# Two products of the output stage in couples of k-blocks, each behind a direct part

## The chip, the core and the metric

The kernel runs on one core of a Trainium2 chip. Its metric is the time of one execution on the device in microseconds (us). The engines named below: TensorE (PE in the profile; PEld is its weight load), VectorE (DVE), ScalarE (ACT), GpSimd (POOL, which here only issues DMAs), and SyncE (SP, whose queue issues the loads).

## The reference

All arrays are float32, with 2048 rows of x, D = 1024 and F = 3584.

```python
def _A_ref(x, dft_seq_re, dft_seq_im, dft_hid_re, dft_hid_im):
    a = jnp.einsum("bsd,ed->bse", x, dft_hid_re)
    b = jnp.einsum("bsd,ed->bse", x, dft_hid_im)
    return jnp.einsum("ts,bse->bte", dft_seq_re, a) - jnp.einsum("ts,bse->bte", dft_seq_im, b)

def _B_ref(x, w1, b1, w2, b2):
    h = jnp.einsum("bsd,df->bsf", x, w1) + b1
    r = jnp.where(h > 0, h, 0)
    h = r * r
    return jnp.einsum("bsf,fd->bsd", h, w2) + b2

g = _sigmoid((x * gate_w).sum(-1, keepdims=True))
return g * a + (1 - g) * b        # a = _A_ref(...), b = _B_ref(...)
```

## The kernel before

**Four stages.** The X stage multiplies x by the two hidden DFT matrices (`ab`), the C stage multiplies that by the two sequence DFT matrices and by g, and keeps the result in DRAM (`gy`). The H stage, in two parts, makes h, squared and rectified, and keeps it in DRAM (`h_far`). The output stage, `o_stage`, multiplies w2 by h (contraction 3584), adds b2, multiplies by 1 - g, adds `gy` and stores. It comes last and is the stage that the change touches. Its result has 8 x 128 rows (D) and 2048 columns.

**Fast multiplication.** Every stage is one 2x2 block product done with seven block products instead of eight (Winograd's form). `SUMS_L` and `SUMS_R` hold the sums of blocks (S1 to S4 of the left, T1 to T4 of the right), `FACTORS` says which factors each product 1 to 7 takes: 1 is (0,0)x(0,0), 2 is (0,1)x(1,0), 3 is S4x(1,1), 4 is (1,1)xT4, 5 is S1xT1, 6 is S2xT2, 7 is S3xT3. `seven` runs the products in the order 1, 2, 5, 6, 3, 7, 4 and says what they are added to: 1 makes `one`; 2 adds to `one` and ends the result block c11; 5 begins c22; 6 adds to `one` and makes `u` and c12; 3 ends c12; 7 adds to `u` and ends c22; 4 adds to `u` and ends c21, the kernel's last result.

**A product.** In the C and output stages (`tall`) the contraction of one block product is cut into `ksteps` k-blocks of 256, 8 in the C stage and 7 in the output stage. An operand is a tile of 128 partitions x 2 x 512 in float32. It is split into `hi` (rounded to fp32r by ScalarE, L220) and `lo` (the rest, by VectorE, L230), each in a slot of its own, and a product of two operands is hi x hi + hi x lo + lo x hi. A step takes one left operand (512 rows) and one right operand (512 columns): 4 row tiles x 2 halves of k x 3 = 24 matmuls of 128x512 into PSUM. A direct product (`direct`) is 7 k-blocks x 2 column halves c = 14 steps in the output stage.

**The second level.** `twice` does 2k of a product's k-blocks once more by seven products. A couple is two neighbouring k-blocks (j = 0, 1); the left operand is cut into two halves of 256 rows (`View`), the right has its two column halves. So a couple takes 7 steps of 12 matmuls, where a direct one takes 4 steps of 24. For that VectorE makes four more sums on each side (L172), 128x512 on the left and 128x1024 on the right, and there are seven left operands of 128x512 (`hi` and `lo` side by side in one slot, `both`) and seven right ones. All couples run a first pass (partial products 1, 6, 7, 5, each added up over the couples), then a second pass (2, 4, 3, added in PSUM onto what the first pass left). What the first pass leaves is taken up by VectorE: when something is already there (`old`), partial product 1 costs a copy of ScalarE and one addition, 6 and 7 two additions each, 5 three. The k-blocks that belong to no couple (`rest`) are done directly; before the change they come last, in half steps of 12 matmuls that go into the same PSUM groups as the second pass (`to`, `own`).

`TWICE_C = {2: 4, 3: 3, 4: 2}` and `TWICE_O = {2: 3, 3: 3}` give the number of couples for each product of the C and the output stage. A direct product 6 also makes `early` the sums T4 of those k-blocks that product 4 needs in couples (L456, L360): T4 is stored to DRAM and loaded again later, where otherwise T2 is stored and T4 is made from the loaded T2 in product 4.

**PSUM.** A `Group` is a set of row tiles added up over some steps; `banks` holds four pools of two banks each. With `onto`, ScalarE first copies the earlier value into PSUM (L293). A finished pair of row tiles goes to `put` (a copy by ScalarE, L432, or `final`) or `add` (VectorE, L438). `final` in the output stage is two scalar_tensor_tensor (L831) and one addition (L834) by VectorE and a store from POOL's queue (L936). The kernel's last block ends by `last` instead, row tile by row tile (`by_row`; L818, L820, stores at L821 from SP's and ACT's queues). An addition of `five` that ends a block has its final made `LATER` = 3 steps on.

**The order of the work** is written by a planner that runs at build time. `steps` is the list of steps in TensorE's order. For each step i, loads are issued up to `LOADS` = 12 steps ahead when there are free slots (55 slots of SBUF in all, some kept back), sums and conversions must be in VectorE's and ScalarE's queues `SUMS` = 3 and `RESTS` = 2 steps ahead of their use, and go up to `SPREAD` = 9 steps ahead where the planner's own clock for VectorE still has room within the present step and slots are free. Each engine then works through its queue in order.

Of the kernel before, what the change touches and what calls it, by code (L numbers as in the profile page):

```python
# [16 lines left out]
NF = F // P  # L17
SLOTS, KEEP, RAWS = 55, 5, 4
WIDE, TALL_C, TALL_O = ((1, 2, 5, 6, 3, 7, 4),) * 3
TWICE_X, TWICE_C, TWICE_O = (1, 2, 5, 3, 4), {2: 4, 3: 3, 4: 2}, {2: 3, 3: 3}  # L20
LATER = 3
WARM = 44
FAR_TALL, FAR_WIDE = ("T2",), ()
TWICE_H = (1, 2, 5, 3, 4), (2, 5, 3, 4)
# [17 lines left out]
def gated_mix_kernel(ctx: ExitStack, tc: tile.TileContext, x4, xn, w4, ct, w1a, w1b, w2, b1, b2, gw, out):  # L42
# [276 lines left out]
    def step(st, mv, group):  # L319
        st.uses += 1  # L320
        mv.uses += 1
        steps.append((st, mv, group, []))
        needs = 0
        count[group] = count.get(group, 0) + 1
        if count[group] % group.k == 0:
            needs += group.done[count[group] // group.k - 1][1]
        wanted.append(needs)
# [81 lines left out]
                    ends[e] = len(steps)  # L409
        return ends  # L410

    def tall(left, right, ksteps, order, second, target, final, last=None):

# [42 lines left out]

        def twice(p, old, new, ends, drop, sign):

            l, r = FACTORS[p]
            k = second[p]
            rest = range(2 * k, ksteps)
            more = len(rest)
            tmp = {key: Near("u") for key in ((0, 0),)}

            def block(m, c):
                return c, m

            def near(b):  # L470
                return b if isinstance(b, Near) else Part(b)

            base = {(j, q): near(left[2 * q + j].of(l)) for j in range(2) for q in range(k)}
            l2 = {q: Sums(lambda m, j, q=q: View(base[j, q], 256 * m), SUMS_L, True) for q in range(k)}
            r2 = {q: Sums(lambda j, c, q=q: right[2 * q + j, c].of(r), SUMS_R, True) for q in range(k)}

            def one(_, ps):
                if old:
                    tmp[0, 0].new()
                    nc.scalar.activation(flat(tmp[0, 0].slot), flat(ps), AF.Copy)  # L480
                    add(new, block(0, 0), ps, src=old)
                    if drop:
                        old[block(0, 0)].drop()
                else:
                    put(new, block(0, 0), ps)

            def onward(dst, key, ps):

                if old:
                    u = tmp[0, 0].slot  # L490
                    nc.vector.tensor_tensor(flat(u), flat(u), flat(ps), op=ADD)
                    at = new[key].slot or new[key].new()
                    nc.vector.tensor_tensor(flat(at), flat(old[key].slot), flat(u), op=ADD)
                    vec(2 * (VEC[0] + VEC[1]))
                    new[key].begun = True
                    if drop:
                        old[key].drop()

            def six(_, ps):
                if old:  # L500
                    onward(new, block(0, 1), ps)
                else:
                    add({block(0, 1): new[block(0, 1)]}, block(0, 1), ps, src={block(0, 1): new[block(0, 0)]})

            def seven_(_, ps):
                if old:
                    onward(new, block(1, 0), ps)
                else:
                    add({block(1, 0): new[block(1, 0)]}, block(1, 0), ps, src={block(1, 0): new[block(0, 1)]})

            def five(_, ps):
                key = block(1, 1)
                add(new, block(0, 1), ps)
                if old:
                    at = new[key].slot or new[key].new()
                    nc.vector.tensor_tensor(flat(at), flat(old[key].slot), flat(ps), op=ADD)
                    if drop:
                        old[key].drop()
                    nc.vector.tensor_tensor(flat(at), flat(at), flat(tmp[0, 0].slot), op=ADD)
                    vec(2 * (VEC[0] + VEC[1]))  # L520
                    tmp[0, 0].drop()
                    new[key].begun = True
                    if ends and not more:
                        new[key].done = True
                        later.append((now[0] + LATER, lambda: final(new[key], None)))
                else:
                    add({key: new[key]}, key, ps, ends and not more, src={key: new[block(1, 0)]})

            fresh = old is not new
            groups = {1: Group(2, k, (one, fresh + bool(old), [new[block(0, 0)]])),  # L530
                      6: Group(2, k, (six, fresh, [new[block(0, 1)]])),
                      7: Group(2, k, (seven_, fresh, [new[block(1, 0)]])),
                      5: Group(2, k, (five, fresh, [new[block(1, 1)], new[block(0, 1)]]))}
            for q in range(k):
                for p2 in (1, 6, 7, 5):
                    l_, r_ = FACTORS[p2]
                    step(l2[q].operand(l_, 256), r2[q].operand(r_), groups[p2])

            def to(m, c):
                key = block(m, c)  # L540
                if last and p == order[-1] and (m, c) == (1, 1):
                    return Group(2, more, (lambda _, ps, row: last(new[key], ps, row), 0, [new[key]]),
                                 onto=[new[key]], by_row=True)
                return Group(2, k * ((m, c) != (1, 1)) + more, (lambda _, ps: put(new, key, ps, ends), 0, [new[key]]),
                             onto=[new[key]])

            groups = {2: to(0, 0), 3: to(0, 1), 4: to(1, 0), None: to(1, 1)}
            for q in range(k):
                again = Sums(lambda j, c, q=q: right[2 * q + j, c].of(r), SUMS_R, True)
                again.made.update({key: r2[q].of(key) for key in ("T1", "T2")})  # L550
                for p2 in (2, 4, 3):
                    l_, r_ = FACTORS[p2]
                    step(l2[q].operand(l_, 256), again.operand(r_), groups[p2])
            own = []
            for q in rest:
                st = left[q].operand(l)
                for c in range(2):
                    mv = right[q, c].operand(r)
                    own += [(Half(st, 256 * m), mv, groups[{(0, 0): 2, (0, 1): 3, (1, 0): 4}.get((m, c))])
                            for m in range(2)]  # L560
            if last and p == order[-1]:
                own.sort(key=lambda e: e[2] is groups[None])
            for e in own:
                step(*e)
# [215 lines left out]
    def c_stage():  # L780
        rows = [Row(n, False) for n in range(2)]
        to = {}

        def target(i, n, k):
            near = Near("y")
            to[near] = i, n, *k
            return near

        def final(dst, ps):
            i, n, c, rp = to[dst]  # L790
            nc.vector.tensor_tensor(dst.slot, dst.slot if ps is None else ps, rows[n].of(c).broadcast_to([P, 2, 512]),
                                    op=ALU.mult)
            vec(VEC[0] + VEC[1])
            rows[n].used()
            stores.append((gy[i, n, c, rp], dst, 0, 2))

        at = len(steps)
        tall(lambda i, j, q: ab[j, q, i], lambda j, n, q, c: ct[n, c, j, q], 8, TALL_C, TWICE_C, target, final)
        return at, rows


    def o_stage():
# [10 lines left out]
        def last(dst, ps, k):  # L813
            i, n, c, rp = to[dst]
            e, t, add = 4 * i + 2 * rp + k, 1024 * n + 512 * c, fetched[i, n, c, rp]
            dst.slot or dst.new()
            at = dst.slot[:, k, :]
            nc.vector.scalar_tensor_tensor(at, ps[:, 0, :], b2c[:, e:e + 1], rows[n].of(c)[:, 0, :], op0=ALU.add,  # L818
                                           op1=ALU.mult)
            nc.vector.tensor_tensor(at, at, add.slot[:, k, :], op=ADD)  # L820
            (nc.scalar if k else nc.sync).dma_start(out[e * P:(e + 1) * P, t:t + 512], at)  # L821
            if k:
                rows[n].used()
                add.used()
                dst.drop()
# [14 lines left out]

        fetched = {}
        at = len(steps)
        ends = tall(lambda i, j, q: w2[i, j, q], lambda j, n, q, c: h_far[j, q, 2 * n + c], 7, TALL_O, TWICE_O, target, final, last)
        return at, rows, fetched, ends

    def want(k, *items):
# [10 lines left out]
    at, rows, fetched, ends = o_stage()  # L857
# [7 lines left out]
    n = len(steps)  # L865
# [138 lines left out]
```

## Time and profile before

| | us |
|---|---|
| median of 3 runs | 1891.29 (1889.42 to 1892.37) |
| the profiled execution | 1888.96 |
| its span, first to last instruction | 1886.9 |
| granted TensorE clock, mean | 0.999 |

The page's second part cuts the span into 40 slices of 47 us and shows the busy share of each in tenths, and the share of the DMA engines:

```profile
PE   9999999999999999999999999999999999999998
DVE  8997898599777998798896997989976997789882
ACT  6474564363343554455484797767954434264440
DMA  5732989339786489383551865628872887629971
```

A row of groups reads: line, engine, operation, out<-in, shape, xcount | busy us in all, mean ns of one | idle us just before them, and what ended it. A row of the timeline reads: start, length, engine, line, operation, count. A row of windows reads: the stretch and its length, then for PE, PEld, DVE, ACT and POOL the busy us and the number of instructions, then the clock, the DMA share and GB/s. A row of waits reads: who waited for whom, us in all, times, the longest.

### The profile page before, as it was taken

To read this page: it belongs to the slowest core of one execution; us is meant where nothing else is said; L and a number is where in the kernel's file an instruction comes from. 1 tells how busy PE (TensorE), PEld (TensorE's weight loads), DVE (VectorE), ACT (ScalarE), POOL (GpSimd) and SP (SyncE) were. 2 spreads that over 40 slices of the span, in tenths; PEclk is the share of its full clock that TensorE was granted. 3 is DMA by queue.
4 is the path that set the end of the run, shared out by engine and by line. 5 is a ranking of instruction groups with operands and counts; after the bars stand their busy time and mean duration, and the time that the engine had idled before them with its cause. 6 is when DMAs were issued, how large, how long until landed. Compare 5 with 4: busy or idle time off the path is not lost.

```text
span 1886.9 us, 21962 instructions
## 1 busy us (share of the span) xinstructions
PE 1876.6 (99%) x8288; PEld 1551.3 (82%) x8288; DVE 1610.3 (85%) x1543; ACT 1001.3 (53%) x1123; POOL 86.8 (5%) x161
## 2 busy tenths in 40 slices
PE   9999999999999999999999999999999999999998
PEld 7888888888888888888888888888888888888887
DVE  8997898599777998798896997989976997789882
ACT  6474564363343554455484797767954434264440
POOL 0000110000010000000000000000100001000000
PEclk9999999999999999999999999999999999999999
DMA  5732989339786489383551865628872887629971
GB/s 223 247 121 86 348 288 412 129 117 375 261 312 256 151 322 383 139 312 112 170 198 56 325 228 195 228 84 299 293 259 97 317 336 265 218 103 370 409 300 45
DMA packets 128425, 442.93 MB, mean 235 GB/s; under 512 B 14128, under 2 KB 23616, under 8 KB 128320
## 3 DMA queue, kind: packets, MB, share of 16 engines
q1 hardware_dynamic: 106416, 363.26, 53.0%
q0 software_dynamic: 21472, 77.61, 10.3%
q8 instruction: 65, 1.06, 0.2%
q10 hardware_dynamic: 432, 0.66, 0.1%
q14 instruction: 40, 0.33, 0.1%
HBM read 362.83 MB, written 78.65 MB: 234 GB/s over the span
## 4 chain that ended last, share of the span: by engine, by line
PE 97%; DVE 2%; ACT 0%; DMA 0%; issue 0%; SPq 0%; DVEq 0%; ACTq 0%
PE ps L306 97%; DVE lo L230 1%; DVE h L603 0%; DVE sum L172 0%; DMA raw<-in_w 0%; DVE o L818 0%; ACT u L596 0%; ACT hi L220 0%; DVE o L820 0%; DVE raw L172 0%; SPq L152 0%; DVEq L172 0%; DVEq L230 0%; ACTq L596 0%
## 5 line engine op out<-in xcount | busy, mean ns | idle before, releaser
L306 PE MATMUL ps<-hi 128*128 128x512 f32 x2328 | 905.7, 390 | 4.0 <-ACT hi L220 3.6
L306 PE MATMUL ps<-lo,hi 128*128 128x512 f32 x2328 | 905.3, 389 | 0.0
L306 PE MATMUL ps<-hi,lo 128*128 128x512 f32 x2328 | 904.2, 389 | 0.1
L220 ACT ACTIVATE hi<-raw 128x1024 fp32r<-128x1024 f32 (+2 forms) x413 | 420.6, 1037 | 399.0 <-DVE raw L172 274.1
L230 DVE TENSOR_TENSOR lo<-raw,hi 128x1024 fp32r<-128x1024 f32 (+2 forms) x413 | 484.5, 1199 | 57.5 <-ACT hi L220 31.3
L306 PEld LDWEIGHTS ps<-hi 128*128 128x128 f32 x2328 | 437.2, 188 | 95.9 <-ACT hi L220 4.2
L306 PEld LDWEIGHTS ps<-hi,lo 128*128 128x128 f32 x2328 | 437.1, 188 | 92.0 <-DVE lo L230 1.0
L306 PEld LDWEIGHTS ps<-lo,hi 128*128 128x128 f32 x2328 | 437.3, 188 | 91.0 <-DVE lo L230 0.4
L172 DVE TENSOR_TENSOR raw<-raw 128x1024 f32<-128x1024 f32 (+1 forms) x276 | 326.4, 1207 | 56.4 <-DMA raw<-in_ct 19.4
L220 ACT ACTIVATE hi<-sum 128x1024 fp32r<-128x1024 f32 (+1 forms) x172 | 176.1, 1036 | 184.8 <-DVE sum L172 151.2
L306 PE MATMUL ps<-hi,both 128*128 128x512 f32 x840 | 259.8, 389 | 0.0
L230 DVE TENSOR_TENSOR lo<-sum,hi 128x1024 fp32r<-128x1024 f32 (+1 forms) x172 | 203.3, 1198 | 32.9 <-PE ps L306 16.6
L306 PEld LDWEIGHTS ps<-hi,both 128*128 128x128 f32 x840 | 157.7, 188 | 33.8 <-ACT ps L293 0.7
L306 PE MATMUL ps<-lo,both 128*128 128x512 f32 x420 | 163.5, 389 | 0.0
L172 DVE TENSOR_TENSOR sum<-raw 128x1024 f32<-128x1024 f32 (+1 forms) x116 | 121.9, 1066 | 35.4 <-PE ps L306 28.1
L172 DVE TENSOR_TENSOR sum<-raw,sum 128x1024 f32<-128x1024 f32 (+2 forms) x87 | 96.8, 1119 | 12.0 <-PE ps L306 11.7
L603 DVE TENSOR_TENSOR h<-h,ps 128x1024 f32<-128x1024 f32 x92 | 98.2, 1086 | 9.6 <-ACT u L596 7.1
L596 ACT ACTIVATE u<-ps 128x1024 f32<-128x1024 f32 x76 | 71.9, 950 | 62.0 <-PE ps L306 54.3
L306 PEld LDWEIGHTS ps<-lo,both 128*128 128x128 f32 x420 | 78.8, 188 | 16.1
L293 ACT ACTIVATE ps<-u 128x1024 f32<-128x1024 f32 (+1 forms) x74 | 70.0, 953 | 22.2 <-DVE o L831 12.0
L700 ACT ACTIVATE h<-h,b1c 128x512 f32<-128x512 f32 x112 | 74.3, 712 | 6.3 <-DVE h L603 6.0
L220 ACT ACTIVATE both<-sum 128x512 fp32r<-128x512 f32 x60 | 37.1, 625 | 52.7 <-DVE sum L172 33.4
(61 smaller groups left out, 650.5 us busy)
## 6 DMA issues: line engine op xcount, KB each, us to landing
raw<-in_ct SPq DMA_DIRECT2D x151, 512.0 KB, 6.2
raw<-h SPq DMA_DIRECT2D x132, 512.0 KB, 7.3
raw<-in_x SPq DMA_DIRECT2D x107, 512.0 KB, 5.3
raw<-in_w SPq DMA_DIRECT2D x98, 512.0 KB, 6.3
raw<-ab SPq DMA_DIRECT2D x72, 512.0 KB, 6.8
h<-h POOLq DMA_DIRECT2D x48, 512.0 KB, 5.7
raw<-in_w1a SPq DMA_DIRECT2D x36, 512.0 KB, 5.0
ab<-ab POOLq DMA_DIRECT2D x32, 512.0 KB, 6.7
```

The lines of the kernel that those rows point to most:

```text
L172: nc.vector.tensor_tensor(self.slot[:, k, c], src[0][:, k, c], src[1][:, k, c], op=self.op)
L220: nc.scalar.activation(self.hi[:, k, c], self.block.slot[:, k, c], AF.Copy)
L230: nc.vector.tensor_tensor(self.lo[:, k, c], self.block.slot[:, k, c], self.hi[:, k, c].bitcast(F32), op=SUB)
L293: nc.scalar.activation(t[:, :n, :], b.slot[:, at:at + n, :], AF.Copy, scale=self.sign)
L306: nc.tensor.matmul(self.ps[r // self.per][:, r % self.per, :], a[:, kk, r * P:(r + 1) * P], b[:, kk, :], start=self.at == 1 and kk + n == ...
L596: nc.scalar.activation(view(near.slot, k), view(ps, k), AF.Copy, scale=float(sign))
L603: nc.vector.tensor_tensor(view(near.slot, k), view((src or dst)[k].slot, k), view(ps, k), op=ADD if sign > 0 else SUB)
L700: nc.scalar.activation(dst.slot[:, k, :], (dst.slot if ps is None else ps)[:, k, :], AF.Relu, bias=b1c[:, tile0 + k:tile0 + k + 1])
```

## The change

`TWICE_O` gets two couples for product 1 and two for product 4. With `FIRST_C = (2,)` and `FIRST_O = (2, 4)`, `twice` does the k-blocks outside the couples first, as whole steps of 24 matmuls in two groups of four row tiles, when there is no earlier value (`not old`, product 1) or the product is in `first`; the sums of these steps are put into the product's own blocks by ScalarE, and the couples then go on from them as their `old`. This holds for products 1, 2 and 4 of the output stage; product 3 keeps its k-block at the end. In the C stage product 2 has no k-block outside its couples, and product 4 isn't in `FIRST_C`.

In product 4, the last, the steps of the second pass are sorted so that partial product 4 comes behind 2 and 3, and the block (1, 0) that it ends goes row tile by row tile through `last`. Before, that was the second column half of the direct product, two blocks of two row tiles each.

As product 4 now has couples, product 6 of the output stage makes T4 early for k-blocks 0 to 3, both column halves.

```diff
-TWICE_X, TWICE_C, TWICE_O = (1, 2, 5, 3, 4), {2: 4, 3: 3, 4: 2}, {2: 3, 3: 3}
+TWICE_X, TWICE_C, TWICE_O = (1, 2, 5, 3, 4), {2: 4, 3: 3, 4: 2}, {1: 2, 2: 3, 3: 3, 4: 2}
 LATER = 3
+FIRST_C, FIRST_O = (2,), (2, 4)
...
-    def tall(left, right, ksteps, order, second, target, final, last=None):
+    def tall(left, right, ksteps, order, second, first, target, final, last=None):
...
             k = second[p]
             rest = range(2 * k, ksteps)
+            if rest and (not old or p in first):
+                some = [Group(4, len(rest), (lambda rp, ps, c=c: put(new, (c, rp), ps, sign=sign), 2 * (old is not new),
+                                             [new[c, rp] for rp in range(2)]),
+                              onto=old and [old[c, rp] for rp in range(2)], spend=drop) for c in range(2)]
+                sts = {q: left[q].operand(l) for q in rest}
+                for q in rest:
+                    for c in range(2):
+                        step(sts[q], right[q, c].operand(r), some[c])
+                old, rest, drop = new, (), False
             more = len(rest)
...
-                if last and p == order[-1] and (m, c) == (1, 1):
-                    return Group(2, more, (lambda _, ps, row: last(new[key], ps, row), 0, [new[key]]),
+                if last and p == order[-1] and (m, c) == ((1, 1) if more else (1, 0)):
+                    return Group(2, more or k, (lambda _, ps, row: last(new[key], ps, row), 0, [new[key]]),
                                  onto=[new[key]], by_row=True)
...
+            own = []
             for q in range(k):
                 again = Sums(lambda j, c, q=q: right[2 * q + j, c].of(r), SUMS_R, True)
                 again.made.update({key: r2[q].of(key) for key in ("T1", "T2")})
                 for p2 in (2, 4, 3):
                     l_, r_ = FACTORS[p2]
-                    step(l2[q].operand(l_, 256), again.operand(r_), groups[p2])
+                    own.append((l2[q].operand(l_, 256), again.operand(r_), groups[p2]))
+            if last and p == order[-1] and not more:
+                own.sort(key=lambda e: e[2] is groups[4])
+            for e in own:
+                step(*e)
...
-        ends = tall(lambda i, j, q: w2[i, j, q], lambda j, n, q, c: h_far[j, q, 2 * n + c], 7, TALL_O, TWICE_O, target, final, last)
+        ends = tall(lambda i, j, q: w2[i, j, q], lambda j, n, q, c: h_far[j, q, 2 * n + c], 7, TALL_O, TWICE_O, FIRST_O, target, final, last)
```

More of the change, by code (lines that the diff above doesn't have):

```diff
@@ L797, in c_stage @@
         at = len(steps)
-        tall(lambda i, j, q: ab[j, q, i], lambda j, n, q, c: ct[n, c, j, q], 8, TALL_C, TWICE_C, target, final)
+        tall(lambda i, j, q: ab[j, q, i], lambda j, n, q, c: ct[n, c, j, q], 8, TALL_C, TWICE_C, FIRST_C, target, final)
         return at, rows
```

## The prediction

> **What bounds the kernel now.** I read the page's head, then PE's waits, then the chain of waits, then a table of windows, one for each of the output stage's seven products (their bounds are counted back from the last matmul: products 1, 2, 5, 6, 3, 7, 4 have 336, 300, 336, 336, 300, 336, 336 matmuls).
>
> ```profile
> span 1886.9 us, 21962 instructions
> PE 1876.6 (99%) x8288; PEld 1551.3 (82%) x8288; DVE 1610.3 (85%) x1543; ACT 1001.3 (53%) x1123; POOL 86.8 (5%) x161
> ...
> PE ps L306 <- ACT hi L220: 3.6, 2, 2.9
> PE ps L898 <- DVE ones L895: 1.1, 1, 1.1
> PE ps L306 <- ACT ps L293: 0.3, 1, 0.3
> ...
> 1300.11 577.56 PE ps L306 x2546
> ```
>
> TensorE sets the time: it waited 5.0 us in the whole execution, and the chain's last piece is 2546 matmuls end to end: 577.56 / 2546 = 0.2268 us each. Fewer matmuls are therefore worth 0.2268 us apiece, as long as the others keep up. VectorE, at 85%, is the one that may not:
>
> ```profile
> core 0: us, PE busy (x) PEld busy (x) DVE busy (x) ACT busy (x) POOL busy (x), PEclk, DMA share, GB/s
> 1364.80:1440.80 76.00, 76.00 (x337) 62.90 (x337) 49.07 (x51) 34.81 (x42) 2.15 (x4) 1.00 0.58 211
> 1440.80:1508.80 68.00, 68.00 (x301) 56.20 (x300) 63.85 (x67) 34.72 (x40) 0.98 (x2) 1.00 0.66 247
> 1508.80:1585.00 76.20, 76.20 (x338) 63.07 (x337) 62.70 (x56) 31.86 (x31) 5.13 (x9) 1.00 0.79 293
> 1585.00:1661.20 76.20, 76.20 (x338) 63.10 (x337) 56.02 (x54) 26.19 (x30) 4.23 (x8) 1.00 0.61 217
> 1661.20:1729.20 68.00, 68.00 (x301) 56.16 (x300) 66.85 (x72) 38.99 (x45) 1.08 (x2) 1.00 0.65 244
> 1729.20:1805.40 76.20, 76.20 (x338) 63.08 (x337) 64.38 (x59) 33.52 (x33) 1.81 (x3) 1.00 0.94 364
> 1805.40:1881.70 76.30, 76.30 (x337) 62.81 (x335) 44.00 (x45) 16.76 (x18) 4.28 (x6) 1.00 0.44 168
> ```
>
> PE is busy for the whole of each window. VectorE is nearly full in the two products that already use the second level (2 and 3: 94% and 98%), and has 26.9 us free in product 1 and 32.3 us in product 4, the two that are changed.
>
> **The change part by part.**
>
> *Matmuls.* Product 1 was 14 steps of 24 matmuls. Now six steps (k-blocks 4 to 6) stay direct, 6 x 24 = 144, and two couples take 2 x 7 steps of 12 = 168: 312 instead of 336. Product 4 likewise. Product 2 keeps its 300 and only does its direct part first. So 48 matmuls go: 48 x 0.2268 = **-10.9 us**. Beyond that nothing can be gained, since PE has no idle time in these windows.
>
> *VectorE's work.* Its prices:
>
> ```profile
> 1367.85 19.39 DVE L230 TENSOR_TENSOR lo<-raw,hi 128x1024 fp32r<-128x1024 f32 x17
> ...
> 1398.98 1.29 DVE L230 TENSOR_TENSOR both<-sum,both 128x512 fp32r<-128x512 f32 x2
> ...
> L438 DVE TENSOR_TENSOR o<-o,ps 128x1024 f32<-128x1024 f32 x11 | 13.4, 1219 | 11.6 <-ACT u L432 7.9 <-PE ps L306 2.7 <-ACT u L480 1.0
> L230 DVE TENSOR_TENSOR both<-raw,both 128x512 fp32r<-128x512 f32 x18 | 12.3, 688 | 0.0
> ```
>
> A row of one instruction overlaps the next by a little: (19.39 - 1.22) / 16 = 1.14 us from start to start for 128x1024, 1.29 - 0.69 = 0.60 for 128x512; an addition out of PSUM lasts as long as the first kind. A couple done directly takes six rests lo, 6 x 1.14 = 6.8. By the second level it takes 4 sums and 7 rests on the left, 11 x 0.60 = 6.6, and 4 sums and 7 rests on the right, 11 x 1.14 = 12.5: 12.3 more, 24.6 for two couples. Taking up the seven partial products (1 addition, then 2, 2 and 3) is 8 x 1.14 = 9.1. So each of products 1 and 4 costs VectorE **33.7 us more**.
>
> *Products 1, 2 and 5.* Free time of VectorE: 26.9 + 4.2 + 13.5 = 44.6; less the 5.4 that PE becomes shorter, 39.2, against 33.7. It fits over the three. Over 1 and 2 alone it doesn't: 31.1 - 5.4 = 25.7, that is 8.0 short. What may slide from 2 into 5 are the finals of product 2 and the first operands of product 5. Product 2's direct part first also helps: 10.9 us of PE with three rests to make. So the stall lies between 0 and 8.0; I take **+2.0**, near the lower end, as the window of product 3 went at 98% without a wait of PE. Whether the free time of product 1 can be used is the open point. There VectorE stood before tiles whose slot PE had not released:
>
> ```profile
> DVE sum L172 <- PE ps L306: 16.5, 9, 3.9
> ACT both L220 <- PE ps L306: 8.8, 3, 4.6
> ```
>
> (the waits between 1381 and 1460 us). All 55 slots were taken, because the 21 operands of product 1, two slots each, had been prepared far ahead: the row of 17 rests above ends at 1387, while PE read the last of them after 1430. With only nine direct operands, 18 slots, that hoard becomes smaller, and the couples' first operands can be made from about 1378 on, 19 us before their step at 1397. So I expect it to be usable.
>
> *Products 6 and 4.* `early` makes 8 of the 14 sums T4 in product 6 and sends them out and back; the same number of T2 copies is no longer stored for them, and loads only move (8 more in product 6, 8 fewer later). 8 x 1.14 = 9.1 us of VectorE goes from 4 into 6, where 20.2 are free. Product 4 then has 44.0 + 33.7 - 9.1 = 68.6 in 70.9, and product 7 before it has 11.8 free. The nearest case is product 4 of the C stage, which already is two couples with early T4, with PE as busy:
>
> ```profile
> 791.90:873.60 81.70, 81.70 (x361) 67.37 (x360) 77.82 (x72) 40.81 (x43) 3.19 (x6) 1.00 0.67 245
> ```
>
> 77.8 of 81.7 and no wait. One place is new: sorted for the last block, the second pass runs 2, 3, 2, 3, 4, 4, so group 3 begins one step of 12 x 0.2268 = 2.7 us after the fourth partial product, and needs VectorE's addition (1.22) and ScalarE's copy back into PSUM at L293 (1.02, the row below) by then. That fits with 0.5 to spare, unless VectorE is two instructions late (2.3 us, so a wait of 1.8). Behind that copy on ScalarE stand the next hi conversions. I take **+0.3** (0 to 1.8).
>
> *ScalarE, queues, loads.*
>
> ```profile
> L293 ACT ACTIVATE ps<-u 128x1024 f32<-128x1024 f32 x62 | 63.3, 1023 | 18.2 <-DVE o L831 8.0 <-DVE y L791 4.3 <-DVE h L603 3.0
> L220 ACT ACTIVATE hi<-sum 128x1024 fp32r<-128x1024 f32 x156 | 163.3, 1056 | 175.6 <-DVE sum L172 144.2 <-PE ps L306 16.3 <-DMA gy<-y 5.5
> L220 ACT ACTIVATE both<-sum 128x512 fp32r<-128x512 f32 x60 | 37.1, 625 | 52.7 <-DVE sum L172 33.4 <-PE ps L306 18.9
> ```
>
> A couple's conversions take 7 x 0.63 + 7 x 1.06 instead of 6 x 1.06, 5.4 more; with seven more copies into and out of PSUM at 1.02, product 1 (and 4) asks 18 us more of ScalarE: 53 of 70.6, hidden. Product 2's moved part gives VectorE as many additions as before and ScalarE seven more copies (four blocks put aside, three fetched again), 7.2 on 34.7 of 68; its two steps' loads go to the front of that product on SP's queue, ahead of the couples'. Product 1 loads four right blocks twice, 1.4 us each (512 KB at the 364 GB/s of product 7, an estimate), beside a DMA share of 0.58. On POOL's queue T4 copies replace T2 copies one for one, and are wanted only two products later.
>
> *The end.*
>
> ```profile
> 1877.69 0.75 DVE L818 SCALAR_TENSOR_TENSOR o<-ps,b2c,g 128x512 f32<-128x512 f32 x1 [28.69 <-PE ps L306]
> ...
> 1881.86 0.74 DVE L818 SCALAR_TENSOR_TENSOR o<-ps,b2c,g 128x512 f32<-128x512 f32 x1
> 1882.64 0.69 DVE L820 TENSOR_TENSOR o<-o,raw 128x512 f32<-128x512 f32 x1
> ...
> 1883.36 0.34 ACTq L821 DMA_DIRECT2D out<-o  x1
> ...
> out<-o ACTq DMA_DIRECT2D x2, 256.0 KB, 2.5
> ...
> out<-o POOLq DMA_DIRECT2D x2, 512.0 KB, 3.1
> ```
>
> VectorE was idle 28.7 us before the last four rows; now it works until about 8 us before the end, and only two rows are left to the row-wise path. The last row's two instructions and its store stay as they are. The block before them ends 24 matmuls = 5.4 us earlier, takes 2 x 0.75 + 1.22 = 2.7, and its store by POOL lands 3.1 us after issue (when little else moves, as 35 us before the end), 0.4 us behind the last matmul; the last row's, issued at 1883.36, lands 2.5 us on, 4.1 behind it. **0** (0 to 1).
>
> *Sum* against the profiled execution's own 1888.96 (span 1886.9): -10.9 + 2.0 + 0.3 = -8.6, so 1880.4. That execution was 2.3 us quicker than the median of the runs, 1891.29; on the median's footing the forecast is **1882.7**.
>
> The C stage is built by the same function, but its product 2 has four couples of eight k-blocks and no direct part, and its product 4 isn't in FIRST_C, so nothing moves there.
>
> **The rivals.**
>
> *A. VectorE is short in products 1 and 2, and what could slide doesn't.* Then PE waits 8.0 us, if in one place then with a slower clock behind it:
>
> ```profile
> 14.91 0.80 PE L306 MATMUL ps<-hi 128*128 128x512 f32 x1 [2.91 <-ACT hi L220]
> ...
> 18.14 0.40 PE L306 MATMUL ps<-hi,lo 128*128 128x512 f32 x1
> ```
>
> After a wait of 2.9 us the next seven matmuls took 3.23 us instead of 1.59, 1.6 lost. -10.9 + 8.0 + 1.6 + 0.3 gives 1890.3. For it: the 98% of product 3 leaves no reserve. Against: the nearby free time of product 5. [...]
>
> *B. Slower: the free time of product 1 stays free, because slots and not VectorE set the pace there.* A couple holds sums, both passes' blocks and operands at once, and a step lasts 2.7 us instead of 5.4, so the same number of prepared steps covers half the time. Each us of the 26.9 that can't be used adds to the 8.0. Half unused: 8.0 + 13.5 = 21.5, so 1891.3 - 10.9 + 21.5 + 0.3 = 1902.2. It is slower by over 0.2% once waits exceed 14.7, that is when more than 6.7 of the 26.9 are lost. For it: the waits for slots above. Against: product 2, three couples at once, had only 4.2 us free.
>
> *C. Nothing stalls:* 1880.4, within the forecast's own range.
>
> *D. The matmuls go, but product 4's second pass waits,* VectorE finishing its 68.6 us late: it must be done about 8 us before the end, 68.6 - 8 = 60.6 in 62.9. If product 7 hands over 5 us less than before, 3 us of wait: 1885.4.
>
> **How the numbers follow.** Forecast with C and D's smaller part 0.60, D 0.06, A 0.18, B 0.16. 0.2% (3.8 us) is about what a measurement of this kernel tells from no change. Faster: forecast and D, 0.66. Same: A, 0.18. Slower: B, 0.16. The range goes from 1879 (no stall, and 1.4 for the spread of the runs) to 1893, taking in A and leaving out most of B.
>
> **What would show it.** Right: about 8196 matmuls on PE beside the 44 of the start; products 1 and 4 in 70.8 us each; VectorE over 95% in products 1 and 2; PE's waits in the output stage under 4 us; VectorE idle before the last rows for a few us. Wrong: PE waits for lo or hi in product 1 with VectorE waiting for PE (B), or with VectorE full (A); a wait at L293 in the last 20 us (D).

## The result, and the profile after

| | before | changed |
|---|---|---|
| median of 10 runs each, us | 1890.91 (1889.05 to 1892.37) | 1886.49 (1883.10 to 1890.02) |
| ratio to before | | 0.9977, 95% interval 0.9968 to 0.9986 |
| profiled execution, us (span) | 1888.96 (1886.9) | 1884.27 (1882.3) |

The changed kernel is faster by 0.23%, 4.4 us in the medians, with an interval of 2.6 to 6.0 us. The forecast was 1882.7, 8.6 us under the median known then; the range, 1879 to 1893, holds the result. What is new is the spread: 6.9 us from the quickest run to the slowest, against 3.3 before.

The page's head and PE's waits in the changed kernel:

```profile
span 1882.3 us, 22015 instructions
PE 1868.7 (99%) x8240; PEld 1545.3 (82%) x8240; DVE 1674.7 (89%) x1622; ACT 1039.7 (55%) x1176; POOL 87.5 (5%) x162
...
PE ps L307 <- ACT hi L221: 3.4, 1, 3.4
PE ps L307 <- ACT ps L294: 2.7, 3, 1.8
PE ps L915 <- DVE ones L912: 1.1, 1, 1.1
PE ps L307 <- DVE lo L231: 0.8, 2, 0.6
```

8240 - 44 = 8196 matmuls: the 48 are gone. The waits for PSUM reloads (ACT at L294, the old L293) have grown from 0.3 to 2.7 us. The windows of the output stage's seven products and of the end show where:

```profile
core 0: us, PE busy (x) PEld busy (x) DVE busy (x) ACT busy (x) POOL busy (x), PEclk, DMA share, GB/s
1367.05:1438.84 71.79, 71.13 (x314) 58.45 (x312) 70.41 (x77) 47.58 (x61) 2.15 (x4) 1.00 0.62 213
1438.84:1506.89 68.05, 68.05 (x301) 56.22 (x300) 67.82 (x76) 41.09 (x49) 1.22 (x2) 1.00 0.64 227
1506.89:1583.05 76.16, 76.16 (x337) 63.10 (x336) 70.46 (x63) 32.98 (x32) 3.83 (x7) 1.00 0.88 340
1583.05:1659.21 76.16, 76.16 (x337) 63.10 (x336) 59.19 (x56) 27.84 (x31) 5.33 (x10) 1.00 0.71 268
1659.21:1729.69 70.48, 68.57 (x301) 56.26 (x300) 69.78 (x77) 37.95 (x45) 1.10 (x2) 1.00 0.61 228
1729.69:1805.85 76.16, 76.16 (x337) 63.12 (x336) 64.08 (x59) 33.56 (x33) 1.79 (x3) 1.00 0.95 367
1805.85:1876.57 70.72, 70.72 (x313) 58.42 (x311) 69.54 (x77) 34.81 (x42) 5.00 (x7) 1.00 0.34 122
1876.57:1882.30 5.73, 0.16 (x1) 0.00 (x0) 1.74 (x3) 0.00 (x0) 0.00 (x0) 0.79 0.43 158
```

Each window runs from a product's first matmul to the next product's. Less 0.2268 for each matmul, what is left is what PE lost there: product 1, 71.79 - 312 x 0.2268 = 1.0; product 3, which the change doesn't touch, 70.48 - 300 x 0.2268 = 2.4; all others under 0.1. VectorE is now full in products 1, 2, 3 and 4 (98%, 100%, 99%, 98%).

The spans differ by 4.6 us: -10.9 for the matmuls, +1.0 and +2.4, about +0.4 at the end, and +2.7 in the X stage, which the change doesn't reach, less 0.3 for an earlier first matmul. The experiments put the X stage's part to chance.

**The wait in product 3.** VectorE and ScalarE there, first in the kernel before, then in the changed one. The first pass of product 3 ends 144 matmuls after its beginning, at 1693.8 before and at 1691.9 after.

```profile
1693.13 1.22 DVE L491 TENSOR_TENSOR u<-u,ps 128x1024 f32<-128x1024 f32 x1
1694.26 1.22 DVE L438 TENSOR_TENSOR o<-o,ps 128x1024 f32<-128x1024 f32 x1
1695.39 1.22 DVE L493 TENSOR_TENSOR o<-o,u 128x1024 f32<-128x1024 f32 x1
...
1695.51 1.03 ACT L293 ACTIVATE ps<-o 128x1024 f32<-128x1024 f32 x1 [3.66 <-DVE o L438]
```

```profile
1692.71 1.22 DVE L503 TENSOR_TENSOR u<-u,ps 128x1024 f32<-128x1024 f32 x1
1693.85 1.22 DVE L231 TENSOR_TENSOR lo<-raw,hi 128x1024 fp32r<-128x1024 f32 x1
1694.98 1.22 DVE L505 TENSOR_TENSOR o<-o,u 128x1024 f32<-128x1024 f32 x1
1696.12 1.22 DVE L440 TENSOR_TENSOR o<-o,ps 128x1024 f32<-128x1024 f32 x1
...
1696.29 1.03 ACT L294 ACTIVATE ps<-o 128x1024 f32<-128x1024 f32 x1 [2.59 <-DVE o L505]
...
1695.12 0.50 PE L307 MATMUL ps<-lo,both 128*128 128x512 f32 x1 [0.16 <-DVE lo L231]
1697.37 0.50 PE L307 MATMUL ps<-hi,both 128*128 128x512 f32 x1 [1.75 <-ACT ps L294]
```

Before, the copy into PSUM that the second pass needs first after its own first step begins 1.7 us behind the first pass and is done at 1696.54, just as that step of 12 x 0.2268 = 2.72 us ends. After, it begins 4.4 us behind: an operand's rest (lo at 1693.85) stands between the additions, and the additions come in another order (the source asks for groups 2, 4, 3 in both kernels, but in the built program the second pass of product 3 begins with groups 2, 3, 4 before and 2, 4, 3 after). From one matmul's start to the next 2.3 us pass.

### The profile page after: what moved, and what is told of

Same layout as the page of the kernel before. It is cut to its first block, busy times and chain, and to the rows that moved or that the text cites. A ratio compares the mean times of both kernels' runs of the same rounds, so it can differ in the third digit from the quotient of the medians.

```text
span 1882.3 us, 22015 instructions
## 1 busy us (share of the span) xinstructions
PE 1868.7 (99%) x8240; PEld 1545.3 (82%) x8240; DVE 1674.7 (89%) x1622; ACT 1039.7 (55%) x1176; POOL 87.5 (5%) x162
## 4 chain that ended last, share of the span: by engine, by line
PE 94%; DVE 4%; DMA 1%; issue 0%; ACT 0%; SPq 0%; DVEq 0%; ACTq 0%
PE ps L307 94%; DVE lo L231 1%; DVE sum L173 1%; DVE h L620 0%; DMA raw<-in_x 0%; DMA g<-g_far 0%; DVE both L231 0%; DVE u L503 0%; DVE raw L173 0%; DMA raw<-in_w 0%; DVE o L505 0%; DVE o L440 0%; SPq L153 0%; ACT ps L294 0%; DVE o L835 0%
## 5 line engine op out<-in xcount | busy, mean ns | idle before, releaser
L307 PE MATMUL ps<-hi 128*128 128x512 f32 x2200 | 857.2, 390 | 3.7 <-ACT hi L221 3.4
L307 PE MATMUL ps<-hi,lo 128*128 128x512 f32 x2200 | 856.5, 390 | 0.7 <-DVE lo L231 0.6
L307 PE MATMUL ps<-lo,hi 128*128 128x512 f32 x2200 | 857.0, 390 | 0.0
L307 PEld LDWEIGHTS ps<-hi 128*128 128x128 f32 x2200 | 414.0, 188 | 90.4 <-ACT hi L221 3.8
L307 PEld LDWEIGHTS ps<-lo,hi 128*128 128x128 f32 x2200 | 413.7, 188 | 85.8 <-DVE lo L231 0.3
L307 PE MATMUL ps<-hi,both 128*128 128x512 f32 x1064 | 329.8, 390 | 2.4 <-ACT ps L294 2.4
L307 PEld LDWEIGHTS ps<-hi,both 128*128 128x128 f32 x1064 | 199.9, 188 | 45.6 <-ACT ps L294 4.1
L307 PE MATMUL ps<-lo,both 128*128 128x512 f32 x532 | 207.4, 390 | 0.2 <-DVE lo L231 0.2
L173 DVE TENSOR_TENSOR sum<-raw 128x1024 f32<-128x1024 f32 (+2 forms) x132 | 136.8, 1053 | 18.2 <-PE ps L307 14.2
L294 ACT ACTIVATE ps<-u 128x1024 f32<-128x1024 f32 x79 | 76.8, 979 | 21.5 <-DVE o L848 7.1
L717 ACT ACTIVATE h<-h,b1c 128x512 f32<-128x512 f32 x112 | 74.4, 714 | 6.0 <-DVE h L620 5.6
```

The lines of the kernel that those rows point to most:

```text
L173: nc.vector.tensor_tensor(self.slot[:, k, c], src[0][:, k, c], src[1][:, k, c], op=self.op)
L294: nc.scalar.activation(t[:, :n, :], b.slot[:, at:at + n, :], AF.Copy, scale=self.sign)
L307: nc.tensor.matmul(self.ps[r // self.per][:, r % self.per, :], a[:, kk, r * P:(r + 1) * P], b[:, kk, :], start=self.at == 1 and kk + n == ...
L717: nc.scalar.activation(dst.slot[:, k, :], (dst.slot if ps is None else ps)[:, k, :], AF.Relu, bias=b1c[:, tile0 + k:tile0 + k + 1])
```

## The experiments

All were timed against the kernel before. "Lost" is worked out as above, in the one profiled execution; that of e5 is the quickest of its five runs, that of e11 the slowest.

| kernel | median, us | ratio (95%) | lost in products, us |
|---|---|---|---|
| e1, product 1 alone | 1887.39 | 0.9983 (0.9974 to 0.9992) | 2: 1.3; 3: 1.2 |
| e2, product 4 alone | 1885.15 | 0.9972 (0.9960 to 0.9983) | 3: 0.4 |
| e3, product 2's part first, alone | 1889.75 | 0.9997 (0.9988 to 1.0005) | none |
| e4, the changed kernel again | 1885.75 | 0.9976 (0.9966 to 0.9985) | 1: 0.5; 3: 4.1 |
| e5, second pass sorted everywhere | 1883.79 | 0.9962 (0.9950 to 0.9975) | 2: 0.9; 5: 1.2; 3: 0.6; 7: 0.2 |
| e6, T4 not made early | 1890.33 | 0.9999 (0.9989 to 1.0008) | 1: 1.7; 3: 1.1; 4: 6.0 |
| e7, product 1's couples first | 1892.90 | 1.0014 (1.0005 to 1.0023) | 1: 10.8; 3: 4.1 |
| e8, product 4's couples first | 1891.82 | 1.0007 (0.9998 to 1.0016) | 1: 0.6; 3: 2.6; 4: 6.2 |
| e9, sorted in 1 and 3 | 1881.63 | 0.9959 (0.9945 to 0.9973) | 3: 2.6 |
| e10, as e9, product 3's part first | 1885.00 | 0.9976 (0.9967 to 0.9985) | 3: 4.3; 7: 1.2 |
| e11, group 2 ahead in 1 and 3 | 1882.43 | 0.9963 (0.9950 to 0.9976) | 3: 5.1 |
| e12, before, 3 sorted | 1890.04 | 1.0000 (0.9991 to 1.0009) | none |

### The parts one by one

```diff
-... TWICE_O = ..., {1: 2, 2: 3, 3: 3, 4: 2}     FIRST_O = (2, 4)
+... TWICE_O = ..., {1: 2, 2: 3, 3: 3}           FIRST_O = ()        # e1
+... TWICE_O = ..., {2: 3, 3: 3, 4: 2}           FIRST_O = (4,)      # e2
+... TWICE_O = ..., {2: 3, 3: 3}                 FIRST_O = (2,)      # e3
```

> Product 1 in two couples behind its direct part; products 2 and 4 as before the change. Lead theory (VectorE's head start is eaten where product 6 makes T4 early and where product 1's couples are taken up): PE loses about 1 us at product 1's pass change, none in product 3; 24 matmuls fewer, so -5.4 + 1.1 = -4.3 us against the kernel before. Rival, start theory (the X stage's 2.7 us more is brought by the changed program): the X stage loses 7 to 8 us again, and the gain is -1.6 us.

> Product 4 in two couples behind its direct part, with T4 early in product 6; products 1 and 2 as before the change. Lead theory: product 3 loses 2 to 2.5 us at its pass change as in the changed kernel, product 1 nothing; -5.4 + 2.4 + 0.4 = -2.6 us. Rival (product 3's wait comes from the lead lost in products 1 and 2, not from product 6): product 3 loses nothing, -5.0 us. Start theory: 2.7 us less gain than either.

> Product 2 with its direct part first and nothing else of the change; the count of matmuls is that of before. Lead theory: no wait in the output stage, within 0.5 us of before. Rival (the moved part itself costs, by its seven more ScalarE copies): 1 us or more slower, with a wait in products 2 or 5.

> The changed kernel once more. Lead theory: 1.1 us lost in product 1 and 2.4 in product 3 again, and the X stage loses anything between 5 and 8 us by chance, so about -6.5 us against before on average if the start is the same for both. Start theory: the X stage loses 7.5 us again, -4.4 us.

The start theory falls: the X stage lost 5.7, 5.7, 7.0 and 6.4 us in these four and 5.0 to 7.8 in all the profiles of this study, with no couples in e3 (7.0) and in the kernel before (5.0). It is chance, and no part of the change. Part of it is the clock: near the start, 3.41 us went at half clock in the kernel before, which lost 5.0, and 6.83 us in the first profile of the changed kernel, which lost 7.7.

Neither part alone does what the lead theory expected. Product 4 alone costs product 3 only 0.4 (2 to 2.5 were expected) and is worth 5.0 us in the median: the rival's number. The rival's reason (all of product 3's wait comes from products 1 and 2) isn't right either. Product 1 alone costs product 3 1.2 us, but by another wait. In e1 VectorE's additions are done in time; ScalarE stands 1.3 us before a load of h, and the copy into PSUM that PE needs next is queued behind that conversion:

```profile
1692.02 1.03 ACT L294 ACTIVATE ps<-o 128x1024 f32<-128x1024 f32 x1 [1.30 <-DVE o L440]
1694.33 1.06 ACT L221 ACTIVATE hi<-raw 128x1024 fp32r<-128x1024 f32 x1 [1.28 <-DMA raw<-h]
1695.30 1.01 ACT L294 ACTIVATE ps<-o 128x1024 f32<-128x1024 f32 x1
...
1696.36 0.50 PE L307 MATMUL ps<-hi,both 128*128 128x512 f32 x1 [0.90 <-ACT ps L294]
```

e2's 0.4 is a wait of the changed kernel's kind, behind late additions; its full 2.4 us came only with both parts. In the medians the parts alone are worth 2.7 us (e1) and 5.0 us (e2), together 4.4 in both series: the whole change can't be told apart from its product 4 alone.

Product 1 alone, without product 2's direct part first, has its wait in product 2 (1.3 us) instead of at its own pass change. The moved part of product 2 is by itself worth nothing (e3). Whether it is what moved this wait isn't shown, as e1 leaves out product 4's couples too.

e4 also shows something that can widen the spread of the changed kernel's runs. PE in product 3, then the granted clock around it:

```profile
1693.73 0.50 PE L307 MATMUL ps<-lo,both 128*128 128x512 f32 x1 [0.20 <-DVE lo L231]
1695.98 0.68 PE L307 MATMUL ps<-hi,both 128*128 128x512 f32 x1 [1.75 <-ACT ps L294]
```

```profile
core 0: us, PE busy (x), PEclk, DMA share, GB/s
1693.50:1696.13 2.63, 0.68 (x3) 1.00 0.70 246
1696.13:1699.55 3.42, 3.42 (x9) 0.50 0.02 7
1699.55:1703.00 3.45, 3.45 (x17) 1.00 0.40 128
```

The same 2.3 us from one matmul's start to the next, but here the clock is granted at half for the 3.42 us behind it: 9 matmuls, where the 3.45 us of the next row have 17. 2.4 us of waiting become 4.1. In the first profile of the changed kernel the same gap cost no clock (granted at 1.00 from 1694 to 1702).

The length of the gap doesn't tell the two cases apart. e9 and e11 below show it again: PE waits 1.6 us for a lo in product 3 in both, and behind that wait the matmuls begin 0.23 us apart in e9, and up to 0.43 in e11. What decides between the two isn't shown.

Over all runs the mean clock of the changed kernel is lower too:

| | runs | mean clock | at 0.999: us | at 0.996: us |
|---|---|---|---|---|
| before (three series) | 74 | 0.9986 | 1889.8 (48 runs) | none |
| changed (two series) | 20 | 0.9975 | 1882.7 (4 runs) | 1888.6 (5 runs) |

Before rounding the means differ by 0.0012, and 0.0012 of 1886 us is 2.2 us. The changed kernel's runs at 0.999 are 7.1 us under those of before, near -10.9 + 1.0 + 2.4 = -7.5. Where the half-clock stretches of the unprofiled runs lie isn't recorded. The one behind product 3's wait costs 1.7 us and came in one of two profiles, so it can't be all of the 2.2. The stretch at the start (3.41 us before, 6.83 in the changed kernel's first profile) is chance, as the X stage's losses above, and half clock behind the last matmul (1.8 us of the span before, 2.4 in that profile) lowers the mean and costs nothing.

### Each behind its direct part

```diff
-                if p == 6 and q < 2 * second.get(4, 0):
+                if p == 6 and q < 2 * second.get(4, 0) and not last:     # e6
-            if rest and (not old or p in first):
+            if rest and p in first:                                      # e7
-FIRST_C, FIRST_O = (2,), (2, 4)
+FIRST_C, FIRST_O = (2,), (2,)                                            # e8
```

> The changed kernel, with the eight sums T4 made in product 4 from a reloaded T2 in place of early in product 6. Lead theory: product 3's wait falls from 2.4 or more to 1.2 us, as with product 1 alone in couples, and product 4, which then asks VectorE for 78 us in 70.9, loses 3 to 7 us. Rival (product 6's work has no part in it): product 3 loses 2.4 us or more as before.

> The changed kernel, with product 1's couples ahead of its direct part. VectorE makes four additions fewer (4.6 us), but the first couple needs 12.3 us of VectorE in its first 10.9 us, behind the H stage's full queue. Lead theory: PE waits in product 1 for lo or hi operands, 4 to 10 us in all, partly at half clock; slower than the changed kernel by 3 to 9 us. Rival (the direct part first is no help): the same time as the changed kernel, or up to 2 us less.

> The changed kernel, with product 4's couples ahead of its direct part (which then ends in half steps, its last block row tile by row tile). VectorE is full through product 7's finals when the first couple comes, so the lead theory expects a wait of 1 to 4 us at the start or pass change of product 4, against none in the changed kernel. Rival (product 4 has room either way): within 1 us of the changed kernel.

PE's waits at the two places, in e7 and e8:

```profile
1373.73 0.80 PE L307 MATMUL ps<-hi,both 128*128 128x512 f32 x1 [5.39 <-ACT both L221]
```

```profile
1831.71 0.80 PE L307 MATMUL ps<-hi,both 128*128 128x512 f32 x1 [2.91 <-ACT ps L294]
```

All three lost where the lead theory had it. In e7, without its direct part ahead, product 1's first couple waits 5.4 us for operands. The theory's reason, VectorE's queue, isn't what the trace shows. VectorE itself stands 4.1 us before ScalarE, which has waited 3.8 us for a store of h and then has the H stage's work (L717) between its conversions:

```profile
1365.96 1.06 ACT L221 ACTIVATE hi<-raw 128x1024 fp32r<-128x1024 f32 x1 [3.77 <-DMA h<-h]
1367.87 1.93 ACT L717 ACTIVATE h<-h,b1c 128x512 f32<-128x512 f32 x3
...
1370.78 1.23 DVE L231 TENSOR_TENSOR lo<-sum,hi 128x1024 fp32r<-128x1024 f32 x1 [4.08 <-ACT hi L221]
```

Behind PE's wait the first matmuls begin 0.59 and 0.43 us apart (1373.73, 1374.32, 1374.75), against 0.23 ahead of it, and shorter waits follow. Product 1 loses 10.8 us (4 to 10 were expected), and the whole gain is gone. Product 4's couples first lose 6.2 at the pass change, more than the 1 to 4 expected, again with slower matmuls behind the wait (0.43 us from start to start, against 0.23 ahead of it). The order within the products is thus worth more than the matmuls saved.

In e6 product 4 asks too much of VectorE. The windows of products 6 and 4:

```profile
1583.00:1659.00 76.00, 76.00 (x337) 62.94 (x336) 53.02 (x50) 26.62 (x29) 3.71 (x7) 1.00 0.52 194
...
1803.60:1880.40 76.80, 72.46 (x313) 57.87 (x311) 76.76 (x84) 35.16 (x42) 4.30 (x6) 1.00 0.41 151
```

VectorE is busy for 76.76 of 76.80 us, PE loses 6.0, and 2.1 more come at the end. Product 3's wait falls to 1.1, as expected, and what is left is e1's wait behind a load of h (1.2 us on ScalarE). So the early T4 does cost product 3, about 1.4 of the 2.4 us, and is still much the better choice. Why product 6 with 20 us free can't take 9 without a trace is shown by VectorE's waits in it, in the changed kernel and then in the one before:

```profile
DVE raw L173 <- DMA raw<-h: 8.8, 3, 6.5
DVE raw L173 <- DMA raw<-in_w: 7.2, 3, 4.7
```

```profile
DVE raw L172 <- DMA raw<-in_w: 4.6, 4, 1.5
DVE sum L172 <- DMA raw<-h: 2.8, 1, 2.8
...
DVE raw L172 <- DMA raw<-h: 0.9, 3, 0.4
```

VectorE there waits 16.0 us for loads, 8.3 before. Its busy time in product 6 rose by 3.2 us only, for 9.1 of added work; in product 3's window, 2.5 us longer, it rose by 2.9, from 66.85 to 69.78. So work that was to be made ahead slid into product 3. Not all of it is the early T4: e2, which has it without product 1's couples, shows 1.4 us more there than before, and e1, the other way round, 1.1.

### The second pass in another order

```diff
+            if last and p in (1, 3):
+                own.sort(key=lambda e: (2, 4, 3).index(next(k for k in groups if groups[k] is e[2])))   # e9, e10, e12
+            elif last and p in (1, 3):
+                own.sort(key=lambda e: e[2] is not groups[2])                                          # e11
```

e5 sorts every product of `tall` so (the last by 2, 3, 4); e10 adds 3 to `FIRST_O`; e12 is e9 with `TWICE_O = {2: 3, 3: 3}` and `FIRST_O = ()`, otherwise the kernel before.

> The changed kernel with the second pass of every product in couples sorted by block (all couples' steps of one group, then the next group), so that two or three steps lie between the first pass and the second reload of PSUM. Pass-change theory (what PE waits for in products 1 and 3 is the chain VectorE addition, ScalarE copy into PSUM): the waits of 1 and 2.4 us vanish, no half-clock stretch follows, and the time is 10 us under the kernel before with a spread of its runs like the one of before (3 to 4 us, not 7 to 8). Rival (VectorE as a whole is short, so the wait is only moved): PE loses 3 to 4 us elsewhere in products 1 to 5, and the time stays at -4 to -5 us.

> The changed kernel with the second pass sorted by block in products 1 and 3 of the output stage alone, so that the ends of product 2 and of the C stage's products keep their order. Pass-change theory: product 1 loses nothing, products 2 and 5 nothing (their 2.1 us in the kernel sorted everywhere came from product 2's finals and operands in their new order), product 3 about 0.6 us; no half clock behind them, so about -10 us against before, with runs within 4 us of each other. Rival (VectorE is short by about 3 us whatever the order): 2 to 3 us lost in products 2 to 5 again, -7 us.

> As the kernel before, and product 3 does its seventh k-block first too. That gives VectorE 10.9 us of PE for three rests ahead of its couples, at the price of seven more ScalarE copies. Lead theory: product 3 loses nothing; -10.5 us. Rival (a direct part first in product 3 takes VectorE's lead from product 7 behind it, as it shrank to 1 to 2 us at the start of product 5 behind product 2): 0.5 to 3 us lost at the start of product 7.

> The changed kernel with only the steps of partial product 2 moved ahead in the second pass of products 1 and 3; 4 and 3 alternate as before. Pass-change theory: these two to three steps (5.4 to 8.2 us) are enough for the second reload, so products 1 and 3 lose under 0.5 us each and the time is that of the kernel sorted in 1 and 3, within 1 us. Rival (operands, not the reload): 2 us or more lost in product 3.

> The kernel before the change with product 3's second pass sorted by block and nothing else. There PE doesn't wait in product 3, so by the pass-change theory the order is worth nothing: within 0.7 us of before. Rival (the order is good by itself, apart from the change's waits): 1 us or more faster.

In product 1 the pass-change theory holds: with two steps between the pass change and the second reload it loses nothing in e5, e9, e10 and e11, against 0.5 to 1.0. In product 3 it holds only for the reload. PE's waits from 1300 us on in e9:

```profile
PE ps L307 <- DVE lo L231: 2.0, 2, 1.6
PE ps L307 <- ACT ps L294: 0.3, 1, 0.3
```

The wait for the reload has become one for operands, 2.6 us in e9 against 2.4. As to the loss the rival was right: 2.6 us or more are lost whatever the order, in product 3 (e9) or spread over products 2, 5, 3 and 7 (e5, 2.9 in all). e9's median, -8.4, lies between the two theories' -10 and -7. e11 lost 5.1, 1.6 of them in nine matmuls that took 3.64 us behind its wait, though its median came within 1 us of e9's, and e10, meant to give product 3 room, lost 5.5 in products 3 and 7 with waits for operands: both missed. Sorting everywhere (e5) shifts what is short to the seam between products 2 and 5.

e9 has the lowest median of the study, 8.4 us under before, with runs from 1880.3 to 1883.5; e11 can't be told apart from it. It keeps product 3's 2.6 us, but as two gaps (PE waits 0.4 and 1.6 us) with the matmuls 0.23 us apart behind each, and none of its five runs had a clock under 0.998. Set against the changed kernel it saves product 1's 1.0 and about 1 us of clock; the rest of the 4 us between the medians is within the intervals, which overlap. e12 shows that the order alone, where PE doesn't wait, is worth nothing.

## Why the prediction was right, and where it was off

- **The matmuls, -10.9.** Right: 48 fewer, and products 1 and 4 without their waits take 70.7 us. VectorE's added work was 64.4 us, for 2 x 33.7 = 67.4 in the prediction.
- **Products 1, 2 and 5, +2.0.** 1.0 and 0.5 in the two profiles, none of it in 2 and 5. The place was wrong: not operands that come late but the pass change of product 1. That the free time of product 1 could be used was right (VectorE 70.4 of 71.8 us), so rival B fell; e7 shows that it stands only with the direct part first.
- **Products 6 and 4.** "9.1 us of VectorE goes from 4 into 6, where 20.2 are free" is the step that failed. Free time in a window isn't time at VectorE's disposal: 8.3 of product 6's 20.2 us were spent waiting for loads before, 16.0 of 17.0 after, and 2.9 us more work fell into product 3. The sum had no term for product 3 at all, though its row, 98% full, was used as a sign that such a load goes without a wait. It cost 2.4 us, and 4.1 with half clock. Without the early T4 (e6) 1.1 is left, about what product 1's couples alone cost product 3 (e1, 1.2), though the sum had them settled within products 1, 2 and 5.
- **Product 4's pass change, +0.3, and the end, 0.** Product 4 lost nothing. In the profile quoted first the end took 5.7 us instead of 5.3, in e4 5.3.
- **The clock.** Rival A had the price of a half-clock stretch, 1.6 us, but only in case of an 8 us wait. Behind the wait of 2.3 us it was paid in one of the two profiles (1.7 us in e4). The mean clock of all runs is lower by 2.2 us' worth; how much of that lies behind product 3's wait isn't shown.

Put together: -10.9 + 1.0 + 2.4 + 2.2 = -5.3, within the interval of 2.6 to 6.0, if all of the clock's 2.2 is counted. Direction, range and mechanism (fewer matmuls, VectorE as the one that may fall short) were right; the size was twice too large because the shortage showed two products behind the place where I looked, and because the clock was lower. That the waits' sum, 3.4 us in the first profile, is not far from the 2.3 of the sum is luck: most of it lies where the sum had nothing.

## What to carry to other kernels

When work is moved into another stage's free time, ask what that time is spent on (here: waiting for loads), and follow the queue into the next stage that has no reserve; that is where it will be paid, even if the change doesn't touch it. Where partial sums are reloaded into PSUM, put steps that don't need the last result between the end of one pass and the reload; in product 1 that was worth 0.5 to 1.0 us, in product 3, where operands were late as well, nothing. A short stop of TensorE should be priced with the half-clock stretch that may follow (here 1.7 us behind a gap of 2.3 us, in one of two profiles), and a wider spread of the runs (here 6.9 us against 3.3) can be a sign of it.

## What was not expected of the hardware

A gap of 2.3 us from one matmul's start to the next led to 3.42 us of half clock in e4 and to none in the first profile of the changed kernel, with the same instructions. Behind the longer waits (2.9 us in e8, 5.4 in e7) the matmuls were slower too, 0.43 us from start to start. Why the load of h that holds up product 3 in e1, four products behind product 1's couples, comes late stays open: e1 has neither early T4 nor a fuller product 6 (VectorE busy 50.4 us there, 56.0 before).
